# A fused attention and MoE kernel on one core: v on a second DMA queue, a token-major last chunk, and a new order

## The chip, the core and the metric

The kernel runs on one core of one Trainium2 chip. The core has five engines, each with its own in-order instruction stream: TensorE (PE; its weight loads are listed apart as PEld), VectorE (DVE), ScalarE (ACT), GpSimd (POOL) and SyncE (SP). SP does no arithmetic here; it issues DMA transfers, and ACT can issue them too. The metric is the device time of one execution in microseconds (us), and the number to compare is the median of several runs. A profile is one execution taken apart; its own span is a little shorter than its time, since the time holds what lies around the program.

## What is computed

Two layers follow each other. The first is a linear attention: q and k are each projected by two small matrices S1 and S2 (8 x 32), and the outer product of the two projections (64 numbers) takes the place of q or k. The second is a gated layer over 4352 tokens, with 2048 hidden units and one beta for each.

```python
def phi(x):
    a = np.einsum('rd,bhsd->bhsr', S1, x)
    b = np.einsum('rd,bhsd->bhsr', S2, x)
    return np.einsum('bhsi,bhsj->bhsij', a, b).reshape(*x.shape[:-1], r * r)
q_p, k_p = (phi(q), phi(k))                      # batch 4, heads 4, 1088 tokens, 32 wide
kv = np.einsum('bhsf,bhsd->bhfd', k_p, v)
z = np.sum(k_p, axis=2)
num = np.einsum('bhsf,bhfd->bhsd', q_p, kv)
den = np.einsum('bhsf,bhf->bhs', q_p, z)[..., None] + 1e-06
...
h = x @ w_in                                     # x: 4352 x 128, w_in: 128 x 2048
g = h * (1.0 / (1.0 + np.exp(-beta * h)))
return g @ w_out                                 # w_out: 2048 x 128
```

## The kernel before

The kernel scales w_in by beta and w_out by 1/beta once (`winp`, `woutp`, in 16 bits), so that the gated layer becomes a product, a silu and a product.

**The order.** The program is written out by hand as a list of short names, `SEQ` (line 842). Each name is a function that issues a few instructions; the list is walked once, at the end of the kernel. Every engine runs its own instructions in the order of the list, and semaphores keep the data dependences. So the list decides, for each engine, what stands behind what.

**Names.** The digit after the letters is the batch, a second digit a part of it. Small letters and capitals of the same name are the same work on different engines.

- Loads: `lk`, `lq`, `lv` bring k, q and v of a batch (`load_rows` line 143, `load_v` line 158), `lb` beta spread over all partitions, `li` w_in, `lo` w_out, `lp` beta for `woutp`, `l1` and `l2` S1 and S2. All go through SP's queue, except `l1`. v is loaded in four pieces of 32 partitions each.
- `h` is one idle matmul into a part of a PSUM tile that nobody reads (line 263); `ci`, `c0`, `c1` make constants.
- `sm` spreads S over the partitions (line 283), `sk` multiplies it with a 0/1 mask for pairs of heads (DVE, line 300), `sw` copies it, `s2` makes blocks of S2.
- k: `tk` transposes k of a batch on DVE (line 446), `kp` projects it on PE (line 465), `ka` transposes the result back (line 516), `o` (POOL) and `O` (DVE) make the outer products in five parts (line 488). `gr`, `gc`, `wp`, `wm`, `wc` make from k the weights of the denominator.
- q: `tq`, `qp`, `qa` in the same way, `DM`/`dm`, `DR`, `DI`, `DS`/`ds` multiply, sum, invert and scale for the denominator (capitals on DVE, small on POOL), `p` (POOL) and `P` (DVE) make the outer products, `t` transposes them on DVE (line 700).
- kv: `v` accumulates k's outer products with v on PE (line 774 for batch 0, line 745 for the others), `kt` and `kc` take it out of PSUM, `nd` deals it to other partitions by six transfers on SP's queue.
- The attention output: `n` (line 715; for batch 0, `f` turns the outer products with PE, `m`/`M` copy them, and `n0` is line 828), and `x` (ACT) or `X` (DVE) copies it into `xT`, the gated layer's input (lines 726 and 840).
- The gated layer: tokens are cut into ten chunks of 256 or 512. `W` is a wave (line 384): two or four units of 128 hidden channels into a PSUM tile of 1024 columns, of which there are two. `S` is its silu on ACT into a buffer `g` (line 401), `V` the second product (line 416), accumulated over all 16 units, with w_out stationary and g moving. `y` transposes a finished chunk on DVE (line 434), and `z` stores it in pieces of 32 partitions, 128 bytes for each token and piece (line 360). There are 68 W, 68 S and 68 V. `u`/`U` make `winp` (line 324), `g`, `e`, `a` make `woutp` on POOL, DVE and ACT.

The first wave needs `x00` and the first half of `winp`; the first V needs the first four blocks of `woutp`; a chunk of batch 1 needs `n1`.

Of the kernel before, what the change touches and what calls it, by code (L numbers as in the profile page):

```python
# [19 lines left out]
def kernel(  # L20
# [39 lines left out]

# [97 lines left out]
    def load_v(b):  # L158
# [3 lines left out]
        for g in range(4):  # L162
            nj = min(NJK, T - NJK * g) if b == B - 1 else NJK
            SP.dma_start(
# [134 lines left out]
    def pair_s():  # L299
        DVE.tensor_tensor(  # L300
            out=sk, in0=cut(sps["t"], [[R, 2], [0, 2], [1, R]]), in1=cut(hm, [[0, 2], [R, 2], [1, R]]), op=MUL
        )
# [50 lines left out]
    def store(o_sb, t0, nt, queues):  # L353
        c = t0
        while c < t0 + 32 * nt:
# [3 lines left out]
            for g4 in range(4):  # L359
                queues[g4 % len(queues)].dma_start(  # L360
# [37 lines left out]
    def silu():  # L398
        ci, j0, jn, per, tw, wv = moe["silu"].pop(0)
        g = sbG.tile([P, 2, TCH], F16, tag="g", name="g")  # L400
        ACT.activation(out=g, in_=wv, func=ACTF.Silu)  # L401
# [7 lines left out]
    def w2():  # L409
        ci, j0, jn, g = moe["todo"].pop(0)  # L410
        t0, tw = tok_chk[ci]
        if j0 == 0:
            moe["acc"] = one("moeout") if ci in ALT else acc("moeout")
        for jj in range(jn):
            j = j0 + jj
            PE.matmul(  # L416
                out=moe["acc"][:, :tw],
                lhsT=woutp[:, j, :],
                rhs=g[jj],
                start=(j == 0),  # L420
                stop=(j == NJ - 1),
            )
# [6 lines left out]
    def turn_out():  # L429
# [4 lines left out]
        DVE.transpose(out=o_sb[:, :nt, :].rearrange("p t d -> p (t d)"), in_=t[:, :tw])  # L434
# [455 lines left out]
```

## Time and profile before

| | us |
|---|---|
| median of 3 runs | 113.21 |
| the runs | 113.64, 110.37, 113.21 |
| the profiled execution's own time | 112.63 |
| its span | 110.8 |
| PE busy in the span | 100.0 |
| ACT busy | 73.5 |
| DVE busy | 63.4 |
| POOL busy | 33.1 |
| mean TensorE clock that was granted | 0.961 of full |

The page of the profile gives the busy time of each engine and, in 40 equal slices of the span, its tenths. Three other views are used: busy time in stretches that one chooses, instructions in order of time (start, duration, engine, line, operation, output and inputs, count; in brackets the idle time before it and what ended it), and the chain of waits, which follows the work that ended last back to the start. Groups of instructions give a count, the busy time, the mean of one in nanoseconds, and the idle time before them. Matmuls are pipelined: a row of a PE group can show more time for one than the distance between two.

### The profile page before, as it was taken

The page shows a single profiled execution, that of the slowest core. Times are in us where ns is not written, and L with a number is a line of the kernel's source. Part 1 is how long each engine was busy: PE and PEld are TensorE (multiplying, and loading weights), DVE is VectorE, ACT ScalarE, POOL GpSimd, SP SyncE. Part 2 cuts the span into 40 slices and gives each one's busy share as a digit, 9 for nine tenths or more (in the row PEclk, how much of TensorE's full clock was granted, in tenths as well). Part 3 has the DMA queues.
Part 4 walks back from the last instruction along what each step waited for, and adds up shares of the span by engine and source line. Part 5 has one row for each costly group of instructions (what it writes and reads, how often), then busy time and mean ns, then how long its engine had stood idle before and what let it go on. Part 6 is the DMA issues. An engine that isn't in the chain of part 4 may idle for free.

```text
span 110.8 us, 2848 instructions
## 1 busy us (share of the span) xinstructions
PE 100.0 (90%) x1183; PEld 55.1 (50%) x1183; DVE 63.4 (57%) x117; ACT 73.5 (66%) x89; POOL 33.1 (30%) x47
## 2 busy tenths in 40 slices
PE   6997779667999988999999999999999999999940
PEld 3453347154274564565755445565545555555730
DVE  3337899999779899909699878375220020020210
ACT  5000001337388993399979966999968999999920
POOL 5000940998009960540681018600000000000000
PEclk9999999975599999999999999999999999999996
DMA  3899999998920100599930015000143405014053
GB/s 84 252 286 214 229 411 321 223 228 254 380 105 6 25 16 6 76 300 213 167 54 10 18 18 87 8 0 11 22 72 61 69 6 94 0 25 70 0 92 50
DMA packets 24316, 12.64 MB, mean 114 GB/s; under 512 B 20464, under 2 KB 22512, under 8 KB 24304
## 3 DMA queue, kind: packets, MB, share of 16 engines
q1 hardware_dynamic: 23744, 12.40, 47.1%
q8 instruction: 9, 0.15, 0.6%
q10 hardware_dynamic: 560, 0.07, 0.4%
q14 instruction: 3, 0.02, 0.1%
HBM read 9.94 MB, written 2.23 MB: 110 GB/s over the span
## 4 chain that ended last, share of the span: by engine, by line
PE 58%; DMA 20%; DVE 15%; issue 1%; SPq 1%; DVEq 0%
PE moeout L416 24%; PE wave L384 23%; DMA beta_bc<-in_moe_beta_dram 11%; DMA v<-in_v_dram 9%; PE nps L715 5%; DVE woutp L338 3%; PE nps L828 2%; DVE qo L488 2%; DVE winp L324 2%; DVE kp L488 2%; PE kps L465 1%; DVE qt L700 1%; PE kvs L745 1%; DVE o_sb L434 1%; DVE qT L446 1%
## 5 line engine op out<-in xcount | busy, mean ns | idle before, releaser
L401 ACT ACTIVATE g<-wave 128x1024 f16<-128x1024 f32 x68 | 65.0, 1049 | 9.7 <-PE wave L384 9.1
L384 PE MATMUL wave<-xT,winp 128*128 128x512 f16 (+1 forms) x160 | 42.2, 362 | 0.7 <-DVE winp L324 0.7
L416 PE MATMUL moeout<-g,woutp 128*128 128x512 f16 (+1 forms) x160 | 38.2, 347 | 0.4 <-DVE woutp L338 0.2
L384 PEld LDWEIGHTS <-winp 128*128 128x128 f16 x160 | 21.3, 147 | 16.2 <-issue 4.3
L434 DVE STREAM_TRANSPOSE o_sb<-moeout 128x512 f32<-128x512 f32 (+1 forms) x10 | 6.3, 632 | 31.8 <-PE moeout L416 31.8
L416 PEld LDWEIGHTS <-woutp 128*128 128x128 f16 x160 | 15.2, 97 | 12.8 <-issue 1.4
L488 POOL TENSOR_TENSOR kp<-kab 128x512 f32<-128x512 f32 (+1 forms) x13 | 15.0, 1174 | 13.9 <-DVE kab L516 8.9
L263 PE MATMUL kvz<-idle 128*128 128x384 f16 x35 | 9.5, 428 | 1.1 <-DVE hm L234 1.1
L488 POOL TENSOR_TENSOR qo<-qab 128x512 f32<-128x512 f32 (+1 forms) x7 | 8.3, 1207 | 6.5 <-DVE qab L684 6.4
L488 DVE TENSOR_TENSOR qo<-qab 128x512 f32<-128x512 f32 (+2 forms) x10 | 10.0, 1003 | 0.1
L700 DVE STREAM_TRANSPOSE qt<-qo 128x512 f32<-128x512 f32 (+1 forms) x12 | 8.7, 742 | 0.0
L542 ACT COPY gt<-gram 128x32 f32<-128x32 f32 x3 | 0.6, 188 | 9.8 <-PE gram L531 9.8
L446 DVE STREAM_TRANSPOSE kT<-k 128x1088 f32<-128x1088 f32 x4 | 5.2, 1297 | 3.0 <-DMA k<-in_k_dram 3.0
L263 PEld LDWEIGHTS <-idle 128*128 128x128 f16 x35 | 4.0, 124 | 5.4 <-issue 3.7
L488 DVE TENSOR_TENSOR kp<-kab 128x512 f32<-128x512 f32 (+1 forms) x7 | 5.7, 807 | 0.0
L446 DVE STREAM_TRANSPOSE qT<-q 128x1088 f32<-128x1088 f32 x4 | 5.2, 1294 | 0.5 <-DMA q<-in_q_dram 0.5
L726 ACT CAST xT<-nps 128x576 f16<-128x576 f32 x6 | 3.8, 638 | 2.3 <-PE nps L715 2.2
L715 PE MATMUL nps<-qt,nd 32*32 32x288 f32 x192 | 5.3, 412 | 0.0
L666 POOL TENSOR_TENSOR qm<-qab 128x288 f32<-128x288 f32 x2 | 1.6, 803 | 12.2 <-DVE qab L660 12.2
L800 PE MATMUL qfps<-ident,qo 128*128 128x128 f32 x18 | 3.2, 314 | 1.8 <-DVE qab L660 1.8
L660 DVE STREAM_TRANSPOSE qab<-qps 128x576 f32<-128x576 f32 x6 | 4.4, 755 | 0.1
L745 PEld LDWEIGHTS kvs<-kp,v 128*32 128x32 f32 x216 | 3.2, 110 | 1.5 <-issue 1.5
(77 smaller groups left out, 67.6 us busy)
## 6 DMA issues: line engine op xcount, KB each, us to landing
k<-in_k_dram SPq DMA_DIRECT2D x4, 544.0 KB, 7.2
q<-in_q_dram SPq DMA_DIRECT2D x4, 544.0 KB, 9.4
v<-in_v_dram SPq DMA_DIRECT2D x15, 144.0 KB, 7.9
...
```

The source lines that it names most:

```text
L263: PE.matmul(out=kvz[:, P:], lhsT=idle, rhs=cut(idle, [[0, 3], [1, P]]), start=fresh, stop=True, skip_group_check=True,)
L384: PE.matmul(out=wv[:, jj // per, o : o + tw], lhsT=unit(j0 + jj), rhs=xT[:, t0 : t0 + tw], start=True, stop=True,)
L401: ACT.activation(out=g, in_=wv, func=ACTF.Silu)
L416: PE.matmul(out=moe["acc"][:, :tw], lhsT=woutp[:, j, :], rhs=g[jj], start=(j == 0), stop=(j == NJ - 1),)
L434: DVE.transpose(out=o_sb[:, :nt, :].rearrange("p t d -> p (t d)"), in_=t[:, :tw])
L446: DVE.transpose(out=dst[:, t0:t1].rearrange("p t s -> p (t s)"), in_=src[:, t0:t1].rearrange("p t d -> p (t d)"),)
L488: eng.tensor_tensor(out=cut(dst[b][:, j0:j1], [[F, n], [R, R], [1, R]]), in0=cut(t, [[step, n], [1, R], [0, R]], j0 * H * step), in1=cut(t ...
L660: DVE.transpose(out=cut(QAB[b], [[4 * R, 2], [4 * R * H, NJK], [1, 4 * R]], 2 * 4 * R * n), in_=PS["qps", b][n][:, :, :JW],)
L700: DVE.transpose(out=QT[b][:, j0:j1].rearrange("p j h c s -> p (j h c s)"), in_=QO[b][:, j0:j1].rearrange("p j h f -> p (j h f)"),)
L715: PE.matmul(out=tiles[g // 2][32 * h : 32 * h + 32, g % 2, : 32 * nj], lhsT=nd_of(b, h, fc, g), rhs=QT[b][rows, :nj, h, fc, :], start=(fc ...
L726: eng(out=cut(x0, [[32 * (QB[2 * i + 1] - QB[2 * i]), 2], [1, 32 * nj]]), in_=PS["num", b][i][:, :, : 32 * nj],)
L745: PE.matmul(out=KVZ[b][32 * h : 32 * h + 32, :F], lhsT=v_t[b][:, h, j, :], rhs=KP[b][:, j, h, :], start=(j == 0), stop=(j == NJK - 1), ski ...
```

## The change

The change has five parts.

1. **Loads.** v of batches 0 and 1 is issued by ACT (`lw0`, `lw1`) in place of SP; the pieces of 32 partitions of every batch come in the order 0, 2, 1, 3 in place of 0, 1, 2, 3. S2 is issued by ACT as S1 was.
2. **The mask of S.** `sk` is two ACT activations with the mask as scale, in place of one DVE product.
3. **The silu buffers.** 24 in place of 18.
4. **The last chunk.** Its silu writes tokens in another order, its second product has g stationary and w_out moving, 128 columns at a time into two PSUM tiles, so that a token lies on a partition; `y` is two DVE copies in place of a transpose, and `z` is two transfers on SP with 512 bytes for each token, in place of two on SP and two on ACT with 128 bytes.
5. **The order.** A new `SEQ`. Several pieces change their engine in it (`O01` to `o01`, `P00` to `p00`, `u0` to `U0` and so on).

```diff
-    sbG = ctx.enter_context(tc.tile_pool(name="sbG", bufs=18))
+    sbG = ctx.enter_context(tc.tile_pool(name="sbG", bufs=24))
...
-    def load_v(b):
+    def load_v(b, gs, eng):
...
-        for g in range(4):
+        for g in gs:
             nj = min(NJK, T - NJK * g) if b == B - 1 else NJK
-            SP.dma_start(
+            eng.dma_start(
...
-        DO[f"lv{b}"] = lambda b=b: load_v(b)
+        if b < 2:
+
+            DO[f"lw{b}"] = lambda b=b: load_v(b, (0, 2, 1, 3), ACT)
+        else:
+            DO[f"lv{b}"] = lambda b=b: load_v(b, (0, 2, 1, 3), SP)
...
     def load_s2():
-        SP.dma_start(out=sr[:, 1], in_=S2)
+        ACT.dma_start(out=sr[:, 1], in_=S2)
...
     def pair_s():
-        DVE.tensor_tensor(
-            out=sk, in0=cut(sps["t"], [[R, 2], [0, 2], [1, R]]), in1=cut(hm, [[0, 2], [R, 2], [1, R]]), op=MUL
-        )
+        for m in range(2):
+            ACT.activation(
+                out=sk[:, :, m, :],
+                in_=sps["t"][:, : 2 * R].rearrange("p (n r) -> p n r", n=2),
+                func=ACTF.Copy,
+                scale=hm[:, m, :1],
+            )
...
-    ALT = {len(tok_chk) - 3, len(tok_chk) - 1}
+    LAST = len(tok_chk) - 1
+    ALT = {LAST - 2}
...
-        ACT.activation(out=g, in_=wv, func=ACTF.Silu)
+        if ci == LAST:
+            ACT.activation(
+                out=cut(g, [[P, 2 * TCH // P], [1, 4], [4, 32]]),
+                in_=cut(wv, [[P, 2 * TCH // P], [32, 4], [1, 32]]),
+                func=ACTF.Silu,
+            )
+        else:
+            ACT.activation(out=g, in_=wv, func=ACTF.Silu)
...
+        if ci == LAST:
+
+            if j0 == 0:
+                moe["acc"] = (two("moeout")[:, 0], one("moeout"))
+            for n in range(tw // P):
+                for jj in range(jn):
+                    j = j0 + jj
+                    PE.matmul(
+                        out=moe["acc"][n][:, :P],
+                        lhsT=g[jj][:, n * P : n * P + P],
+                        rhs=woutp[:, j, :],
+                        start=(j == 0),
+                        stop=(j == NJ - 1),
+                    )
...
+        if ci == LAST:
+            for n in range(tw // P):
+                DVE.tensor_copy(out=o_sb[:, 4 * n : 4 * n + 4, :].rearrange("p t d -> p (t d)"), in_=t[n][:, :P])
+            outs.append((ci, o_sb, t0, nt))
+            return
...
-        store(o_sb, t0, nt, [SP, ACT] if ci == len(tok_chk) - 1 else [SP])
+        if ci < LAST:
+            store(o_sb, t0, nt)
+            return
+        b, r = divmod(t0, S)
+        for n in range(nt // 4):
+            SP.dma_start(
+                out=bass.AP(
+                    tensor=out.tensor,
+                    offset=out.offset + (b * S + r // 32 + 4 * n) * DM,
+                    ap=[[T * DM, 32], [DM, 4], [1, DM]],
+                ),
+                in_=o_sb[:, 4 * n : 4 * n + 4, :],
+            )
```

The order, old and new, up to the attention output of batch 1 (`n1`) and a little beyond:

```diff
-        l1 lk0 l2 ci h0 c0 tk0 h h h h h h h h h h h h h h h c1 h h h sm sw1 sw0 lk1 sk lq0 s2 tk1 h h h
-        h kp0 ka0 o00 tq0 h h h h h o03 h h h kp1 gr0 lv0 gc0 h h wp0 ka1 O01 wm0 qp0 lq1 qc0 lb0 v00
-        qa0 qd0 li0 DMa li1 o02 v01 v02 DRa DIa v03 DSa gr1 P00 tq1 gc1 o04 lb1 DMb h wp1 wc1 v04 DRb f0
-        qp1 DIb m0 DSb kc n00 P01 o10 qa10 P02 qa11 lv1 U2 lk2 U3 h DM1 P03 lp DR1 x00 f1 DI1 u1 u0 m1 W
-        f2 W S W m2 S n01 W o11 o13 S f3 S P04 vz f4 X01 o14 W M3 W v10 O12 v11 v12 S DS1 v13 S v14 p10
-        W p13 S tk2 M4 kt1 p11 lo0 W S kp2 t10 W n02 W rb ka2 X02 lo1 S g7 a0 e2 lq2 g1 S e3 g5 t11 g4 W
-        gr2 V W g6 g9 e8 GC2 lk3 g11 e15 S e12 nd1 a10 S e14 wp2 W WC2 V e13 tq2 V p12 V S t12 W qp2 y
-        t13 qa20 V S V qa21 V V dm2 o20 W n1 tk3 S x10 W V x11 V V W S V W S kp3 DR2 y z O21 ka3 W O23
...
+        l2 ci l1 h0 h h h h h lk0 h c0 c1 lq0 h sm h h h sk lk1 tk0 lw0 s2 h h h h sw1 h h h kp0 h h sw0
+        ka0 h h h tq0 h h gr0 h h o00 gc0 h O02 o01 h h h lq1 wp0 o04 wm0 h qp0 h qc0 tk1 qa0 lb0 h o03
+        qd0 DMa h DRa DIa DMb v00 dsa kp1 v01 h ka1 DRb h h h h gr1 DIb p00 dsb li0 gc1 f0 p03 p04 wp1
+        v02 wc1 lb1 v03 tq1 P01 m0 v04 P02 kc qp1 u1 li1 lp lw1 h qa10 O10 h U0 lk2 h n00 f1 f2 x00 qa11
+        lo0 U3 h lo1 o14 W h h m1 m2 W n01 U2 S W O11 S dm1 f3 lq2 X01 S W f4 rb o12 v10 DR1 S W v11 o13
+        S W v12 DI1 v13 v14 DS1 M3 S p10 lv2 W tk2 W g5 kt1 e0 g1 e7 g4 m4 kp2 n02 g2 S P12 W S W g3 h
+        x02 ka2 S gr2 tq2 S W g15 p13 GC2 S h wp2 t10 W g11 S WC2 e12 a9 V W e13 O20 g6 g14 S t13 V qp2
+        t12 v20 a10 o21 qa20 a8 v21 W p11 qa21 nd1 V t11 S V W O24 o22 n1 y S o23 v22 v23 v24 lk3 tk3 W
+        x10 z x11 V DM2 W S V S V W V DR2 W S V W S S kt2 DI2 V W DS2 V p20 S V t20 W y nd2 kp3 ka3 W
```

The rest of both orders goes on in the same manner and ends with the last S, the last V, `y` and `z`.

More of the change, by code (lines that the diff above doesn't have):

```diff
@@ L347, in invert_beta, with store @@
         DVE.reciprocal(out=rbeta, in_=beta_pu.rearrange("p i u -> p (i u)"))
-    ALT = {len(tok_chk) - 3, len(tok_chk) - 1}
+    LAST = len(tok_chk) - 1
+    ALT = {LAST - 2}
     moe = {"ci": 0, "w": 0, "acc": None, "silu": [], "todo": []}
-    def store(o_sb, t0, nt, queues):
+    def store(o_sb, t0, nt):
         c = t0
@@ L359, in store @@
             for g4 in range(4):
-                queues[g4 % len(queues)].dma_start(
+                SP.dma_start(
                     out=bass.AP(
@@ L411, in w2 @@
         t0, tw = tok_chk[ci]
[L412 to L422, printed above, removed]
+        if ci == LAST:
[11 more added lines that the diff above has]
+                    )
+        else:
+            if j0 == 0:
+                moe["acc"] = one("moeout") if ci in ALT else acc("moeout")
+            for jj in range(jn):
+                j = j0 + jj
+                PE.matmul(
+                    out=moe["acc"][:, :tw],
+                    lhsT=woutp[:, j, :],
+                    rhs=g[jj],
+                    start=(j == 0),
+                    stop=(j == NJ - 1),
+                )
         if j0 + jn == NJ:
@@ L439, in store_out @@
         ci, o_sb, t0, nt = outs.pop(0)
-        store(o_sb, t0, nt, [SP, ACT] if ci == len(tok_chk) - 1 else [SP])
+        if ci < LAST:
[3 more added lines that the diff above has]
+        for n in range(nt // 4):
+            SP.dma_start(
+                out=bass.AP(
[4 more added lines that the diff above has]
+                in_=o_sb[:, 4 * n : 4 * n + 4, :],
+            )
     PS, KP, QO, QT, ND, KAB, QAB, RC, GT, KVZ = ({} for _ in range(10))
@@ L848 @@
-        W p13 S tk2 M4 kt1 p11 lo0 W S kp2 t10 W n02 W rb ka2 X02 lo1 S g7 a0 e2 lq2 g1 S e3 g5 t11 g4 W
-        gr2 V W g6 g9 e8 GC2 lk3 g11 e15 S e12 nd1 a10 S e14 wp2 W WC2 V e13 tq2 V p12 V S t12 W qp2 y
-        t13 qa20 V S V qa21 V V dm2 o20 W n1 tk3 S x10 W V x11 V V W S V W S kp3 DR2 y z O21 ka3 W O23
-        DI2 S O24 o22 V S W V V lq3 S W lv2 V S W ds2 S v20 y v21 v22 v23 P20 v24 t20 P23 p22 W S V W
-        O30 V S kt2 V W V S W P21 gr3 W S V gc3 W t22 S lv3 wp3 S tq3 t23 V W V W t21 V WC3 z y S qp3 S
@@ L853 @@
-        W z o32 nd2 qa30 S V o31 qa31 V dm3 V W n2 V S V x20 x21 DR3 W V DI3 DS3 O34 S z P30 W S V W V W
-        v30 y v31 S W S t30 S o33 p32 P33 V W V W v32 v33 v34 S p31 W kt3 t33 nd3 S V W V z t32 S S W
-        t31 V W V S W S S V W V n3 y S x30 V x31 W V S z V W V S W V W V S W V S W V y S S W V S W S V W
-        V W V z S S W V W S S V W V S W S V W V S W V S W y V W V S S W V W V S W V S W S S V W V z S V
-        V V y z y z
+        l2 ci l1 h0 h h h h h lk0 h c0 c1 lq0 h sm h h h sk lk1 tk0 lw0 s2 h h h h sw1 h h h kp0 h h sw0
@@ new lines @@
+        x02 ka2 S gr2 tq2 S W g15 p13 GC2 S h wp2 t10 W g11 S WC2 e12 a9 V W e13 O20 g6 g14 S t13 V qp2
+        t12 v20 a10 o21 qa20 a8 v21 W p11 qa21 nd1 V t11 S V W O24 o22 n1 y S o23 v22 v23 v24 lk3 tk3 W
+        x10 z x11 V DM2 W S V S V W V DR2 W S V W S S kt2 DI2 V W DS2 V p20 S V t20 W y nd2 kp3 ka3 W
+        p22 V t22 S P21 p23 S t23 O30 W V S W gr3 S lq3 o33 W V S W gc3 V t21 vz tq3 n2 y S z x20 W V
+        lv3 x21 V V W V S W o34 S V W V S o31 wp3 S W O32 V W S WC3 V W v30 y v31 S qp3 qa30 V S W qa31
@@ L858 @@
+        V V W S W S V dm3 V S W v32 v33 DR3 DI3 v34 kt3 DS3 z S W S z V W V V y W S P30 P31 t30 W V S V
+        S W V V W V nd3 S S W p33 V W p32 V t31 S W S S V t33 t32 y n3 V x30 W V x31 S V W V S W V W S V
+        z W S V W V S W V S V S W V z S W V S W V W V S y z W V S W V S W S V y W V S S z W V W S V V S
+        W S V W V S W V W V S V V y S z V y z
     """
```

## The prediction

> **What bounds the kernel now.** I read the 40 slices first, then the engines' busy time in stretches, then the instructions in order of time.
>
> ```profile
> PE   6997779667999988999999999999999999999940
> DVE  3337899999779899909699878375220020020210
> ACT  5000001337388993399979966999968999999920
> POOL 5000940998009960540681018600000000000000
> PEclk9999999975599999999999999999999999999996
> DMA  3899999998920100599930015000143405014053
> ```
>
> Three stages show (slices of 2.77 us, counted from 0). Up to slice 10 the DMA engines are full and ScalarE (ACT) has little to do. From 8 to about 45 us VectorE (DVE) is at nine tenths. From 45 us TensorE (PE) is full, and at the very end ACT is too. The clock row has a dip in slices 8 to 10.
>
> ```profile
> 10.00:15.00 5.00, 2.95 (x67) 1.15 (x69) 4.54 (x9) 0.18 (x1) 3.97 (x4) 1.00 1.03 266
> 40.00:45.00 5.00, 4.33 (x56) 2.44 (x55) 5.00 (x9) 2.46 (x3) 0.72 (x1) 1.00 0.09 16
> 45.60:84.00 38.40, 38.28 (x548) 20.97 (x548) 24.11 (x37) 32.91 (x37) 11.80 (x11) 1.00 0.40 77
> ```
>
> The columns are PE, weight loads, DVE, ACT, POOL (GpSimd), clock, DMA share, GB/s. DVE is busy 4.54 and 5.00 of 5 us in the first two; PE 38.28 of 38.4 in the third. So the end is set twice: by when DVE has prepared batch 1, then by how much work PE has left.
>
> ```profile
> 1.06 6.02 PE L263 MATMUL kvz<-idle 128*128 128x384 f16 x19 [1.06 <-DVE hm L234]
> 4.66 1.31 DVE L446 STREAM_TRANSPOSE kT<-k 128x1088 f32<-128x1088 f32 x1 [2.46 <-DMA k<-in_k_dram]
> 8.34 0.71 PE L465 MATMUL kps<-kT,sk 64*32 64x288 f32 x16
> 10.14 0.81 DVE L516 STREAM_TRANSPOSE kab<-kps 128x288 f32<-128x288 f32 x2
> 15.48 2.06 PE L774 MATMUL kvz<-v,kp 128*64 128x32 f32 x64
> 23.57 0.87 PE L384 MATMUL wave<-xT,winp 128*128 128x256 f16 x4
> 24.80 2.17 DVE L324 TENSOR_TENSOR winp<-w_in_sb,beta_bc 128x512 f16<-128x512 f32 x2
> 45.59 1.60 PE L715 MATMUL nps<-qt,nd 32*32 32x288 f32 x64
> ```
>
> The milestones: the first wave at 23.57; the attention output of batch 1 (`n1`, line 715) at 45.59, just after DVE's last transpose for it. `n1` is my gate: at it the old order has issued 15 W and 8 V, the new one 15 W and 4 V (counted in the two orders).
>
> **The front: -2.6 us.** Start first. In the new order 18 idle matmuls stand ahead of `kp0`; at 6.02/19 = 0.317 us each from 1.06, plus some 0.6 for `sm`, `kp0` starts at 7.4 instead of 8.34 (S lands by then: its loads are first on ACT's queue). `tk1` (1.31) no longer stands ahead of `ka0`, which so ends near 8.9 instead of 10.95: 2.05 earlier, with 1.31 still owed, 0.7 net. Then DVE's load up to the gate:
>
> ```profile
> L488 DVE TENSOR_TENSOR qo<-qab 128x512 f32<-128x512 f32 x7 | 7.0, 1007 | 0.1
> L488 DVE TENSOR_TENSOR kp<-kab 128x512 f32<-128x512 f32 x5 | 4.9, 974 | 0.0
> L338 DVE TENSOR_TENSOR woutp<-w_out_sb,rbeta 128x128 f16<-128x128 f32 x7 | 3.3, 507 | 0.0
> L324 DVE TENSOR_TENSOR winp<-w_in_sb,beta_bc 128x512 f16<-128x512 f32 x2 | 2.2, 1126 | 0.1
> L666 DVE TENSOR_TENSOR qm<-qab 128x288 f32<-128x288 f32 x1 | 0.9, 912 | 0.0
> L840 DVE CAST xT<-nps 128x320 f16<-128x320 f32 x1 | 0.5, 492 | 0.4 <-PE nps L828 0.4
> L300 DVE TENSOR_TENSOR sk<-sps,hm 128x32 f32<-128x32 f32 x1 | 0.2, 192 | 1.8 <-ACT qw L309 1.8
> ```
>
> Off DVE go `DM1` (0.91), three woutp scalings (1.5), and six small ones between 0.19 and 0.49, some 2.1 together (`sk`, `DSa`, `DSb`, `M4`, `X02`, and the first `y`, now behind `n1`): 4.5. On it come `U0` (1.1) and four outer products (`O10 O11 P12 O20`, about 1.0 each) for four that leave (`P00 P03 P04 O12`), one of half size, others partly while POOL was idle; I put 1.1 on that swap. Net 4.5 - 2.2 = 2.3, with 0.7 a gate at 45.59 - 3.0 = 42.6. Against this stands that POOL, which takes what DVE gave, slows DVE's products (the 0.97 mean hides single ones of 0.7 and of 1.3): if each of the nine DVE products from `P01` to `O20` took 0.2 more, 44.4. I take 43.0, -2.6, nearer the first because slices 5, 6 and 10, 11 show POOL with room. Bounds: -4 (all room used) and 0 (POOL becomes what DVE was).
>
> W itself hardly starts earlier. I add up DVE's new order:
>
> ```profile
> 13.37 1.33 DVE L488 TENSOR_TENSOR kp<-kab 128x512 f32<-128x512 f32 x1
> 14.73 0.83 DVE L586 STREAM_TRANSPOSE qab<-qps 128x288 f32<-128x288 f32 x2
> L660 DVE STREAM_TRANSPOSE qab<-qps 128x576 f32<-128x576 f32 x6 | 4.4, 755 | 0.1
> ```
>
> From 8.9: `tq0` 1.3, `O02` 1.3, `wm0` 0.2, `tk1` 1.3, `qa0` 0.8, `qd0` and `DMa` to `DMb` some 1.7 make 15.5; `ka1` 0.8, `DRb` and `DIb` 0.7, `tq1` 1.3, `P01` and `P02` 1.3 each make 20.9; `qa10` 0.8, `O10` and `U0` 0.9 each make 23.5. So the first wave stays at 23.5 to 24. (The loads of win and beta are then long there: the old kernel had them for its use at 20 to 25.) On PE, `gr1`, `f0` and `wp1` follow `ka1`, then 40 of the kv instructions at 2.06/64 us, 1.3 together; `kc` comes near 19.2.
>
> ACT's new work: `sk` as two small activations near 4.4, before any other need for ACT: nothing on the path. Eight issues of v:
>
> ```profile
> 0.74 0.60 ACTq L212 DMA_DIRECT2D sr<-in_S_dram  x1
> 2.48 2.89 SPq L164 DMA_DIRECT2D v<-in_v_dram  x4
> ```
>
> At 0.60 each, `lw0` holds ACT 2.4 us behind `sk` (until 7.2; `gc0` needs `ka0` at 8.9), and `lw1` 2.4 us between `kc` (near 19.2) and `x00`, which so goes at 21.6 while W waits for `U0` at 23.5. Hidden, with 1.5 us of cover; at the old longest spacing SP paid, 2.89/4 = 0.72, still hidden. `m4`, `x02` and one woutp scaling come to ACT (1.1 together), which has room until 84 us. SP is freed of eight issues. The 24 silu buffers do nothing: in the orders silu never leads V by more than 11 before and 12 after, under 18.
>
> **From the gate to the last V: +0.8.** Before, this takes 106.65 - 45.59 = 61.06.
>
> ```profile
> 72.35 0.58 PE kvs L745 x32
> 76.96 0.43 PE wave L384 x2
> 77.39 0.43 PE moeout L416 x2
> 95.15 0.49 PE wave L384 x2
> 84.62 21.36 ACT L401 ACTIVATE g<-wave 128x1024 f16<-128x1024 f32 x23
> 104.64 2.00 PE L416 MATMUL moeout<-g,woutp 128*128 128x256 f16 x16
> 106.67 0.45 DVE L434 STREAM_TRANSPOSE o_sb<-moeout 128x256 f32<-128x256 f32 x1 [1.60 <-PE moeout L416]
> 107.16 0.89 ACTq L360 DMA_DIRECT2D out_dram<-o_sb  x2
> ```
>
> Four V more are owed: 4 x 0.43 = +1.7. The first two parts of batch 2's kv, 32 of its 72 instructions, are done ahead of `n1`: -0.6. The end of the old kernel is bound by ACT (23 silus in a row, 0.93 each), which stretches a wave's pair from 0.43 to 0.49: 23 x 0.05 = 1.2. In the new order ACT is 7 silus ahead of V at `n3`, not 4, with 21 W and 28 V left: PE 21.1 us, ACT 21 x 0.93 + 1.3 = 20.8. PE binds again: -1.2. The last chunk's 16 matmuls of 256 columns (2.00 us, 0.125 each) become 32 of 128, each with its own weight load: between 0 (half the columns, half the time) and +2.0 (no faster each). No row shows one; I take +0.9, the middle. Sum 1.7 - 0.6 - 1.2 + 0.9 = +0.8: last V at 43.0 + 61.06 + 0.8 = 104.9, -1.8.
>
> The Trainium skill ("TensorE: Matmul & The Clock Gate", Back-to-back issue gap) gives about 81 ns for a sustained matmul of 128 columns with its load; by it the 32 would take 2.6 us and the term be +0.6. No row here shows it.
>
> **The tail: -0.3.** The transpose of 0.45 becomes two copies of half the size, the first under PE's last matmuls: -0.2. Two issues on SP stand for two on each of two queues, and packets of 512 B for 128 B: between -0.4 and +0.5 (one issue, 0.45); I take -0.1. The permuted silu output of the last chunk is put at nothing, with a bound of +0.9 (the last silu twice as long).
>
> Sum: -1.8 - 0.3 = -2.1. The profiled execution took 112.63 (span 110.8, 1.83 around it); 112.63 - 2.1 = **110.5**. The median shown is 113.21, of runs from 110.37 to 113.64, so the forecast is 2.4% below the median and 1.9% below the profiled run. About 2% is what a measurement of this kernel can tell from no change.
>
> **Rivals.** *v comes late: slower.* In the new order PE meets `v00` ahead of `kp1`, so all of batch 1 waits for batch 0's v.
>
> ```profile
> 2.48 9.64 DMA v<-in_v_dram
> 9.00:10.00 1.00, 1.00 (x15) 0.61 (x8) 1.00 (x1) 0.00 (x0) 0.00 (x0) 1.00 1.11 207
> 15.00:16.00 1.00, 1.00 (x26) 0.54 (x21) 0.94 (x3) 0.00 (x0) 0.19 (x1) 1.00 1.11 442
> ```
>
> While v moved the engines gave 207 GB/s, after it 442, both with full engines. `ka1` has its turn on DVE at 15.5; `v00` (0.45) and `kp1` (0.72) must precede it, so v has until 14.4. v is issued at 4.8 to 7.2. If both queues got equal bytes, 0.59 MB of v and 0.59 of the others at 207 take 5.7: v is there near 12. If they alternate run by run (1152 B of v, 4352 of k or q, by the lines that load them), 32 pairs for each of 16 engines at 207/16 GB/s take 13.6: from 7.2, 20.8. The old kernel's first product with v stands at 15.48; I take 14. Later, each us costs one: the gain is lost from 16.5, and from 19.4 the median is passed by 2%; at 20.8 the time is 110.5 + 6.4 = 116.9. For it: the full DMA row. Against: the batch-1 loads behind k and q start later than before, and the pieces now alternate halves of the partitions.
>
> The Trainium skill ("DMA: Bandwidth & Descriptors", Issuing engines are not separate DMA queues) says that transfers from ACT and SP run on the same engines and interleave, and that only issue time is saved. That speaks for this rival; the trace, with one small load on ACT's queue, cannot show it.
>
> *The front gains nothing that PE keeps: within 2%.* Gate and V owed cancel: POOL's load eats 1.5 of the 2.3, and the end stays ACT-bound. -2.6 + 1.5 + 1.2 = +0.1 in place of -2.6 in these terms: 112.4 to 113.
>
> *All room is used: much faster.* Gate at -4 and the short matmuls free: 110.5 - 1.4 - 0.9 = 108.2; the clock dip, which more idle matmuls may fill, could give another half us.
>
> **How the numbers follow.** The forecast (109 to 112) 0.45; nothing kept 0.30; more gained 0.11; v late 0.14. The forecast lies on both sides of 110.95, the median less 2%: 0.31 of it faster. Faster 0.31 + 0.11 + 0.02 = 0.44; slower 0.13 of the last; the rest, 0.43, the same. The range leaves out the ends of the two outer cases: 107.5 to 114.8; the forecast's own is 109 to 112.
>
> **What would show it.** `n1` near 43 and the last V near 105; 32 matmuls of about 0.09 in the last chunk; v's first product before 15; waves after 95 us back at 0.43; DVE full to 43 and POOL fuller from 15 to 40. The prediction is wrong if PE idles ahead of line 774, if POOL's outer products are waited for by `t11`, or if ACT still runs without a gap at the end.

## The result and the profile after

The changed kernel takes 123.75 us (median of 4 runs, 122.45 to 124.73), the kernel before on the same chip 112.48 (4 runs, 110.37 to 113.64): a ratio of 1.105, 95% interval 1.074 to 1.136. It is slower by 11 us, where the prediction said 110.5. The profiled execution took 124.49 us, its span 122.7. Medians are of all runs, while ratios and intervals leave out the runs in which the chip was in a slower state (so 1.105 is not 123.75 / 112.48), and where no interval is given too few others were left.

The 40 slices of the changed kernel, of 3.07 us each:

```profile
PE   6894750999799995799996999999999999983630
DVE  3218190397999899972499203519620200102010
ACT  4100100021789994589895897799979999999940
POOL 4006704078578997019081000243000000000000
PEclk9999995589999999999999999999999999999975
DMA  4999999204920151031675200320504050130501
```

Two holes are new. In slice 6 (18.4 to 21.5 us) PE and DVE stand still and POOL is at 4, while the DMA row is full. In slices 36 and 37, PE falls to 3 and 6 while ACT stays at 9. Busy time in stretches (PE, weight loads, DVE, ACT, POOL, clock, DMA share, GB/s) puts numbers to them:

```profile
10.00:15.00 5.00, 2.37 (x37) 1.13 (x35) 2.15 (x5) 0.43 (x3) 4.22 (x4) 1.00 1.00 319
17.00:21.00 4.00, 0.06 (x1) 0.00 (x0) 1.31 (x6) 0.00 (x0) 1.40 (x2) 0.72 1.04 360
104.00:119.00 15.00, 10.04 (x73) 6.60 (x71) 1.73 (x3) 13.81 (x9) 0.00 (x0) 0.96 0.22 35
```

From 10 to 15 us DVE works 2.15 of 5 us, where it worked 4.54 before; from 17 to 21 PE works 0.06 of 4 us; from 104 to 119 PE works 10 of 15 and ACT 13.8. The instructions in order of time (as before) name both causes. First the front:

```profile
5.78 7.06 ACTq L163 DMA_DIRECT2D v<-in_v_dram  x3
8.60 0.72 PE L512 MATMUL kps<-kT,sk 64*32 64x288 f32 x16
13.19 0.38 PE L578 MATMUL gram<-kab 128*32 128x32 f32 x18 [2.63 <-ACT qw L316]
21.18 1.07 PE L821 MATMUL kvz<-v,kp 128*64 128x32 f32 x16 [4.12 <-DMA v<-in_v_dram]
23.50 0.85 DVE L563 STREAM_TRANSPOSE kab<-kps 128x288 f32<-128x288 f32 x2 [5.02 <-PE kps L512]
32.10 0.63 PE L392 MATMUL wave<-xT,winp 128*128 128x256 f16 x4 [0.77 <-DVE qab L707]
50.92 1.67 PE L762 MATMUL nps<-qt,nd 32*32 32x288 f32 x64
```

The issues of v hold ACT until 12.84, not 7.2. The first product with v (`v00`) comes at 21.18, after a wait of 4.12 us for v; before it stood at 15.48. The held ACT is in this too: `gram` waited 2.63 us for the copies behind v's issues, and without the wait for v PE would have come to `v00` at 17.06, 8.5 us after `kp0`. In the kernels below that load v on SP's queue it is 5.7 to 7.7. `kp1` stands behind it on PE, so DVE's `ka1` comes at 23.50 in place of 15.5 in my walk. The first wave is at 32.10 (before 23.57) and `n1` at 50.92 (before 45.59). The chain of waits, read back from the first waves, has two pieces of v in it:

```profile
5.40 7.11 DMA v<-in_v_dram
12.53 8.52 DMA v<-in_v_dram
```

The two pieces join at 12.5 because the kernel's transfers, on both queues together, use eight completion semaphores in turn, and a transfer is issued only when the one eight places before it has landed (read from the trace's semaphore events). v's third piece so waited for k of batch 1 (landed at 7.88) and its fourth for its own first piece (landed at 12.51). The fourth landed at 21.05. Now the end:

```profile
92.38 16.11 ACT L416 ACTIVATE g<-wave 128x1024 f16<-128x1024 f32 x17
108.64 9.31 ACT L410 ACTIVATE g<-wave 128x1024 f16<-128x1024 f32 x4
113.44 0.60 PE L392 MATMUL wave<-xT,winp 128*128 128x256 f16 x4 [1.26 <-ACT g L410]
118.01 1.03 PE L434 MATMUL moeout<-woutp,g 128*128 128x128 f16 x8 [1.65 <-ACT g L410]
```

Seventeen silus take 16.11 us (0.95 each), the last four, of the same 128 x 1024 elements with the permuted output, 9.31 us (2.33 each). Waves wait for them (1.26 us in the row above; a PSUM tile comes free only when its silu is done), and so do the last products.

So the loss has two places, and one measure keeps them apart. Up to `n1` the front counts; from `n1` to the end of the last V, the end. In the changed kernel the second stretch is 119.04 - 50.92 = 68.1 us, before it was 61.06.

### The profile page after: what moved, and what is told of

Same layout as the page of the kernel before. It is cut to its first block, busy times and chain, and to the rows that moved or that the text cites. A ratio compares the mean times of both kernels' runs of the same rounds, so it can differ in the third digit from the quotient of the medians.

```text
span 122.7 us, 2904 instructions
## 1 busy us (share of the span) xinstructions
PE 101.7 (83%) x1212; PEld 57.7 (47%) x1212; DVE 59.1 (48%) x108; ACT 80.3 (65%) x94; POOL 37.1 (30%) x53
## 4 chain that ended last, share of the span: by engine, by line
PE 55%; DMA 15%; DVE 12%; ACT 10%; ACTq 2%; issue 2%; DVEq 0%
PE wave L392 20%; PE moeout L446 19%; DMA v<-in_v_dram 13%; ACT g L410 6%; ACT g L416 4%; PE nps L762 4%; DVE kp L535 3%; DVE qt L747 3%; PE kvz L821 3%; DMA sr<-in_S_dram 2%; PE kvs L792 2%; ACTq L932 2%; DVE woutp L345 2%; DVE qab L707 2%; PE kps L512 2%
## 5 line engine op out<-in xcount | busy, mean ns | idle before, releaser
L416 ACT ACTIVATE g<-wave 128x1024 f16<-128x1024 f32 x64 | 61.2, 1034 | 6.8 <-PE wave L392 6.2
L392 PE MATMUL wave<-xT,winp 128*128 128x512 f16 (+1 forms) x160 | 40.5, 351 | 4.2 <-ACT g L410 2.5
L446 PE MATMUL moeout<-g,woutp 128*128 128x512 f16 (+1 forms) x144 | 36.0, 356 | 0.0
L446 PEld LDWEIGHTS <-woutp 128*128 128x128 f16 x144 | 13.9, 97 | 12.3 <-issue 1.1
L535 POOL TENSOR_TENSOR qo<-qab 128x512 f32<-128x512 f32 (+2 forms) x11 | 13.0, 1194 | 10.6 <-DVE qab L731 10.5
L266 PE MATMUL kvz<-idle 128*128 128x384 f16 x48 | 13.5, 419 | 1.1 <-DVE hm L237 1.1
L410 ACT ACTIVATE g<-wave 128x1024 f16<-128x1024 f32 x4 | 9.3, 2534 | 0.1
L563 DVE STREAM_TRANSPOSE kab<-kps 128x288 f32<-128x288 f32 x8 | 3.4, 462 | 8.2 <-PE kps L512 8.2
L821 PE MATMUL kvz<-v,kp 128*64 128x32 f32 x72 | 3.5, 256 | 4.1 <-DMA v<-in_v_dram 4.1
L535 DVE TENSOR_TENSOR qo<-qab 128x512 f32<-128x512 f32 x6 | 5.9, 1003 | 0.0
L821 PEld LDWEIGHTS kvz<-v,kp 128*64 128x64 f32 x72 | 3.1, 175 | 5.4 <-issue 5.4
```

The source lines that it names most:

```text
L266: PE.matmul(out=kvz[:, P:], lhsT=idle, rhs=cut(idle, [[0, 3], [1, P]]), start=fresh, stop=True, skip_group_check=True,)
L392: PE.matmul(out=wv[:, jj // per, o : o + tw], lhsT=unit(j0 + jj), rhs=xT[:, t0 : t0 + tw], start=True, stop=True,)
L410: ACT.activation(out=cut(g, [[P, 2 * TCH // P], [1, 4], [4, 32]]), in_=cut(wv, [[P, 2 * TCH // P], [32, 4], [1, 32]]), func=ACTF.Silu,)
L446: PE.matmul(out=moe["acc"][:, :tw], lhsT=woutp[:, j, :], rhs=g[jj], start=(j == 0), stop=(j == NJ - 1),)
L535: eng.tensor_tensor(out=cut(dst[b][:, j0:j1], [[F, n], [R, R], [1, R]]), in0=cut(t, [[step, n], [1, R], [0, R]], j0 * H * step), in1=cut(t ...
L821: PE.matmul(out=kvz[64 * c : 64 * c + 64, 32 * m : 32 * m + 32], lhsT=KP[0][:, j, h, :], rhs=v_t[0][:, h, j, :], start=(j == 0 and m == 0) ...
```

## The experiments

The two theories were tested by undoing each alone and both together, then by looking for the mechanism inside each. All times are us. "v00", "n1" and "last V" are starts of the first product with v and of batch 1's attention output, and the end of the last V, in the profiled run.

| run | kernel | median (runs) | before there | ratio, 95% interval | v00 | n1 | n1 to last V |
|---|---|---|---|---|---|---|---|
| before | | 112.48 (4) | | | 15.48 | 45.59 | 61.1 |
| after | | 123.75 (4) | 112.48 | 1.105, 1.074 to 1.136 | 21.18 | 50.92 | 68.1 |
| e1 | after, last chunk as before | 119.21 (4) | 111.67 | 1.068, 1.055 to 1.081 | 23.02 | 51.70 | 62.2 |
| e2 | after, v on SP's queue | 116.14 (4) | 111.67 | 1.041, 1.031 to 1.051 | 15.44 | 43.09 | 67.7 |
| e3 | after, both | 111.08 (10) | 111.67 | none | 13.31 | 40.96 | 62.2 |
| e4 | before, token-major last chunk alone | 116.75 (4) | 111.67 | 1.047, 1.036 to 1.058 | 15.50 | 44.52 | 66.7 |
| e5 | e1, v first on ACT's queue | 112.51 (4) | 111.36 | 1.011, 1.004 to 1.018 | 15.16 | 43.82 | 62.2 |
| e6 | e1, copies ahead of v's issue | 120.97 (4) | 111.36 | 1.087, 1.079 to 1.095 | 22.51 | 52.74 | 62.2 |
| e7 | e2, silu plain, store permuted | 111.23 (4) | 111.36 | none | 14.62 | 42.26 | 62.2 |
| e8 | e2, silu reads permuted | 110.27 (4) | 111.36 | 0.987, 0.977 to 0.997 | 14.16 | 41.81 | 62.2 |
| e9 | e8, 18 buffers | 110.94 (6) | 112.08 | 0.991, 0.980 to 1.001 | 15.04 | 42.69 | 62.2 |
| e10 | e8, pieces 0, 1, 2, 3 | 110.60 (6) | 112.08 | 0.987, 0.977 to 0.998 | 14.57 | 42.22 | 62.2 |
| e11 | before, e8's last chunk alone | 113.13 (6) | 112.08 | none | 15.77 | 45.52 | 61.5 |
| e12 | e8 again | 111.09 (6) | 112.08 | 0.999, 0.993 to 1.005 | 16.63 | 44.28 | 62.2 |
| e13 | e8, six idle matmuls fewer | 109.91 (12) | 111.43 | 0.992, 0.987 to 0.997 | 14.71 | 42.36 | 62.2 |
| e14 | e8 again | 110.46 (12) | 111.43 | 0.990, 0.979 to 1.001 | 14.02 | 41.67 | 62.2 |

### One part undone at a time (e1, e2, e3)

e1 takes part 4 back (plain silu, w_out stationary, transpose, stores of 128 bytes; the kernel before had the last of these on two queues, here all go through SP's). The condition is switched off in the silu, the product, the copies and the store; the first is shown:

```diff
-    ALT = {LAST - 2}
+    ALT = {LAST - 2, LAST}
...
-        if ci == LAST:
+        if False:
...
```

> The changed kernel with the last chunk computed and stored as before (silu without the permutation, w_out stationary, transpose, pieces of 128 bytes; all on SP). Theory A (two separate costs: v of batch 0 comes late, and the last chunk's four permuted silus take 2.3 us each instead of 0.93 while ACT bounds the end): the four silus go back to 0.93, 4 x 1.4 = 5.6 us come back, about 118 us; n1 stays near 50.9. Rival B (the long silus are covered by PE's work, and all of the loss is from the front): 122 or more.

e2 puts v back on SP's queue, at the same place in the order; e3 does both.

```diff
-            DO[f"lw{b}"] = lambda b=b: load_v(b, (0, 2, 1, 3), ACT)
+            DO[f"lw{b}"] = lambda b=b: load_v(b, (0, 2, 1, 3), SP)
```

> The changed kernel with v of batches 0 and 1 issued by SP at the same places of the order, pieces still 0, 2, 1, 3. Theory A: v of batch 0 then stands in SP's queue right behind the second k and lands near 12 to 14 us instead of 21; v00 starts by 15, ka1 by 17 instead of 23.5, n1 near 45 instead of 50.9; about 118 us. Rival C (the new order itself is slow, since POOL and DVE share work badly): v00 is early but n1 stays at 49 or later, 121.5 or more.

> The changed kernel with both: v on SP, and the last chunk as before. What is left of the change is the new order, the two mask activations, S2 on ACT and the 24 buffers. Theory A: the two costs add up, 123.75 - 5.6 - 6 = about 112, no difference from the kernel before within 2 %. Rival C (the order is slow by itself): 116 or more. The prediction's own view of the order, without the two costs: about 110.5.

The order of time of e1, then of e2, then of e3:

```profile
23.02 0.66 PE L821 MATMUL kvz<-v,kp 128*64 128x32 f32 x16 [0.88 <-DMA v<-in_v_dram]
93.17 20.03 ACT L416 ACTIVATE g<-wave 128x1024 f16<-128x1024 f32 x21
```

```profile
15.44 0.66 PE L821 MATMUL kvz<-v,kp 128*64 128x32 f32 x16
100.83 9.31 ACT L410 ACTIVATE g<-wave 128x1024 f16<-128x1024 f32 x4
```

```profile
40.96 1.67 PE L762 MATMUL nps<-qt,nd 32*32 32x288 f32 x64
101.12 2.00 PE L446 MATMUL moeout<-g,woutp 128*128 128x256 f16 x16
```

e1 keeps the late v and loses the slow silus (21 in 20.03 us, 0.95 each); e2 the reverse. From the medians, e1 gives back 123.75 - 119.21 = 4.5 us and e2 123.75 - 116.14 = 7.6; the sum is 12.1, and e3, with both, gives back 12.7. The kernel before read 112.48 beside the changed kernel and 111.67 beside these, so each difference holds to about 1 us. Within that the two costs are separate and add up, and nothing else in the change loses anything of their size: e3's median stands at the time of the kernel before. The forecasts of 118 for e1 and e2 were missed by 1.2 and 1.9 us in opposite directions.

### The late v: issue or rate (e5, e6)

ACT was held by its issues until 12.84, and `sw`, S's copies, stood behind them: `gram` waited 2.63 us for them. So two things could cost: what is queued behind v's issues on ACT, or v itself. e5 (made from e1) leaves v on ACT's queue but issues it right behind S's two loads; e6 (from e1) puts the copies `sw` ahead of v's issues. `gc0`, the copy of `gram`, stays behind them. The edits of e5 and then of e6:

```diff
-        l2 ci l1 h0 h h h h h lk0 h c0 c1 lq0 h sm h h h sk lk1 tk0 lw0 s2 h h h h sw1 h h h kp0 h h sw0
+        l2 ci l1 lw0 h0 h h h h h lk0 h c0 c1 lq0 h sm h h h sk lk1 tk0 s2 h h h h sw1 h h h kp0 h h sw0
```

```diff
-        l2 ci l1 h0 h h h h h lk0 h c0 c1 lq0 h sm h h h sk lk1 tk0 lw0 s2 h h h h sw1 h h h kp0 h h sw0
+        l2 ci l1 h0 h h h h h lk0 h c0 c1 lq0 h sm h h h sk lk1 tk0 sw1 sw0 lw0 s2 h h h h h h h kp0 h h
```

> As e1 (last chunk as before, v on ACT), but with v of batch 0 issued right behind S1, near 2 us, before SP's queue has filled. Compare with e1 (119.2). Theory A (v is late because it is issued behind 3 MB of SP's loads, and its later pieces because each waits for an earlier transfer to land): v lands by 12, v00 starts by 14, n1 near 42, about 112 us. Rival F (a load on ACT's queue gets too small a share beside SP's whatever the time of its issue): v lands after 15, n1 at 45 or later, 115 or more.

> As e1, but the two copies sw0 and sw1 stand ahead of the v issues on ACT, so that the gram of batch 0, which needs the PSUM tile that they free, is not held while ACT waits to issue v. Compare with e1 (119.2). Theory A: the gram runs near 10 instead of 15, but kp1 stands behind v00 and v is as late, so n1 and the time stay within 1 us. Rival G (what costs is ACT held by the issues): n1 2 us earlier or more, 117 or less.

In order of time, e5 and then e6:

```profile
1.67 3.62 ACTq L163 DMA_DIRECT2D v<-in_v_dram  x4
10.43 4.23 POOL L535 TENSOR_TENSOR kp<-kab 128x512 f32<-128x512 f32 x4 [8.29 <-DVE kab L563]
15.16 0.66 PE L821 MATMUL kvz<-v,kp 128*64 128x32 f32 x16 [0.72 <-POOL kp L535]
```

```profile
11.98 0.38 PE L578 MATMUL gram<-kab 128*32 128x32 f32 x18
14.55 0.18 ACT L589 COPY gt<-gram 128x32 f32<-128x32 f32 x1 [8.29 <-DMA v<-in_v_dram]
22.51 1.07 PE L821 MATMUL kvz<-v,kp 128*64 128x32 f32 x16 [5.23 <-DMA v<-in_v_dram]
```

In e6 `gram` came 3.9 us earlier than in e1 (15.83 there) and the time did not fall: it rose from 119.21 to 120.97. So the hold of the copies is covered by the late v. The whole hold is not priced by this, for ACT still came to `gc0` (`gt` above) at 14.55 only, and without the 5.23 us for v PE would have been at `v00` at 17.28, about as late as in the changed kernel. In e1's profile, the longest of its four executions, the hold nearly is the delay: `gram` waited 3.87 us for the copies, and of the time until `v00` at 23.02 only the last 0.88 us is a wait for v.

In e5 the four issues take 3.62 us without a wait, and the time is 6.7 us under e1's, though still above the kernel before (1.004 to 1.018). The pieces land at 8.6, 10.7, 13.2 and 15.1. `v00` starts 0.09 us after the last of them; the row names POOL, but POOL's outer products had ended at 14.66. So v still arrives last there (the rival had it landing after 15, the theory by 12), and yet the time is the theory's: landed at 15.1, it costs little. ACT's queue as such is slow, since the last piece took 10.1 us, and it landed 4.3 us later than the last in e2. What cost 7.6 us was the issue of v on it that late, beside a full queue on SP, with ACT held meanwhile. No run separates the late landing from the hold. The rate shows in the share of the packets. For the changed kernel from 7 to 12.5 us and then from 17 to 21 (q1 is SP's queue, q10 ACT's; packets, MB, share of 16 engines' time):

```profile
q1 hardware_dynamic: 424, 1.56, 82.9%
q10 hardware_dynamic: 200, 0.21, 13.8%
```

```profile
q1 hardware_dynamic: 371, 1.30, 90.2%
q10 hardware_dynamic: 126, 0.13, 11.8%
```

v moved one packet for two to three of SP's, and its packets are a third the size: 0.21 of 1.77 MB (12%) and 0.13 of 1.43 MB (9%). v's last piece of 144 KB took from 12.53 to 21.05, 8.5 us. In e2, with v in SP's queue, its pieces were issued by 4.8 and had landed by 10.8.

### The permuted silu: which side costs (e4, e7, e8)

e4 is the kernel before with part 4 of the change alone. e7 (from e2) has the plain silu and stores the tokens in the other order; e8 (from e2) keeps the permutation but moves the stride from the silu's output to its input.

```diff
-        if ci == LAST:
+        if False:
...
-                    ap=[[T * DM, 32], [DM, 4], [1, DM]],
+                    ap=[[DM, 4], [T * DM, 32], [1, DM]],
```

```diff
-                out=cut(g, [[P, 2 * TCH // P], [1, 4], [4, 32]]),
-                in_=cut(wv, [[P, 2 * TCH // P], [32, 4], [1, 32]]),
+                out=cut(g, [[P, 2 * TCH // P], [4, 32], [1, 4]]),
+                in_=cut(wv, [[P, 2 * TCH // P], [1, 32], [32, 4]]),
```

> The kernel before with part 4 alone: permuted silu, g stationary, two copies, two stores of 512 bytes a token. Theory A: the last four silus take about 2.3 each, ACT bounds the end there, so 112.5 + 5.6 = about 118. Rival B (covered by PE's work): within 1 us of the kernel before. Rival D (the silus are long in the changed kernel because of what PE does beside them there, not because of the permuted output): they stay near 1 us here.

> As e2 (v on SP, last chunk token-major), but the silu of the last chunk writes in order, and the two stores carry the permutation instead (dimensions of 4 and 32 swapped in the output's address). Compare with e2 (116.1) and e3 (111.1). Theory A: the silus go back to 0.93, 5 us come back: 110.5 to 111.5, and the token-major end is worth less than 1 us either way. Rival D (the long silus come from the stationary g and its two PSUM tiles): they stay at 2.3, 116.

> As e2, but the last chunk's silu reads PSUM in the permuted order (innermost 4 elements 32 apart) and writes g in order. Compare with e2 (116.1). If the scattered 16-bit write is what costs (theory A): silus near 1.0, about 111. Rival H (any innermost run of 4, on either side, costs): they stay above 1.8, 114 or more.

The last silus of e4, and then the last silus and products of e8:

```profile
101.15 9.37 ACT L403 ACTIVATE g<-wave 128x1024 f16<-128x1024 f32 x4
```

```profile
99.54 3.77 ACT L410 ACTIVATE g<-wave 128x1024 f16<-128x1024 f32 x4
101.96 2.02 PE L434 MATMUL moeout<-woutp,g 128*128 128x128 f16 x32
```

e4 shows the cost without any of the rest: 9.37 us for four, 5.1 us more than the kernel before. In e8 the same tokens in the same order come at 0.94 us for each silu: reading 32-bit PSUM with a stride of 32 elements costs nothing, writing 16-bit values with a stride of 4 elements costs 1.4 us for 1024 elements of each partition. The 9.31 - 3.77 = 5.5 us appear whole in the stretch from `n1` to the last V (67.7 in e2, 62.2 in e8). e7 has the plain silu too, and its median is the kernel before's; its two last stores took 2.5 us each from issue to landing, against 2.0 and 1.9 in e8.

### The small parts (e9, e10, e11, e12)

e9 and e10 change e8 in a number and a list; e11 is e4 with e8's silu; e12 is e8 again.

```diff
-    sbG = ctx.enter_context(tc.tile_pool(name="sbG", bufs=24))
+    sbG = ctx.enter_context(tc.tile_pool(name="sbG", bufs=18))
```

```diff
-            DO[f"lw{b}"] = lambda b=b: load_v(b, (0, 2, 1, 3), SP)
+            DO[f"lw{b}"] = lambda b=b: load_v(b, (0, 1, 2, 3), SP)
         else:
-            DO[f"lv{b}"] = lambda b=b: load_v(b, (0, 2, 1, 3), SP)
+            DO[f"lv{b}"] = lambda b=b: load_v(b, (0, 1, 2, 3), SP)
```

> The kernel of e8 (v on SP's queue, last chunk token-major with the silu reading permuted and writing in order) with 18 silu buffers in place of 24. The prediction's statement: silu never leads V by more than 12 in the new order, so buffers 19 to 24 are never needed: 110.3 us, the same as e8 within 1%. Rival, the buffers let ACT run ahead near the end: waves or silus wait for a free buffer, and the time is 111.5 or more.

> The kernel of e8 with v's four pieces of 32 partitions loaded in the order 0, 1, 2, 3 as before, in place of 0, 2, 1, 3. Theory that the order of the pieces does nothing: 110.3 us, v's last piece of batch 0 landed within 1 us of e8's, the same first product with v within 0.3 us. Rival, neighbouring pieces share DMA engines or memory ports and move more slowly (207 GB/s stood in the kernel before while v moved): v's last piece lands 2 us later or more, v00 moves to 17 or later, and the time to 112 or more.

> The kernel before (its loads, its order, 18 buffers) with the token-major last chunk alone, its silu reading PSUM permuted and writing in order: e4 with its slow write taken away. If the write's stride was all of e4's 5.1 us, its four last silus take 0.94 us each and the time is that of the kernel before, 111.4, or up to 1 less (the tail: 512-byte stores). Rival, the token-major chunk costs something else too (its stores land later, its 32 short matmuls): 112.5 or more. The difference to e12 on the same chip is what the new order with its mask on ACT and its piece order is worth: 2 us or more if the prediction's front term holds at the end, under 1 if the end eats it.

> The kernel of e8 once more, as it was, beside the three others. 110.3 us, 0.987 of the kernel before; if e8's gain was chance, 111.3 and a ratio of 1.0. n1 near 41.8, the last V near 104.

e9, e10 and e12 lie within 0.5 us of one another: the six buffers and the order of the pieces are worth nothing that these runs can tell (v's last piece landed at 11.6 in e10, at 11.5 in e12). e11, with the old loads and order, stands 2.0 us above e12 by the medians of six runs each, and 1.0 above the kernel before, where the theory had it equal. Its lowest run, 110.94, lies among e12's (110.75 to 112.47), and without an interval neither difference is shown. Its four silus take 0.96 us each, and its stretch from `n1` is 61.5, so the token-major chunk with a clean write costs or gains little.

e12's gain was smaller than e8's (0.999 against 0.987), in intervals that overlap. Its profile is of its longest execution, 112.47, and cannot explain the median, but it shows what moves one execution. In order of time, e12, and under it e3, which has the same front:

```profile
5.56 0.40 PE L286 MATMUL sps<-ident,sr 8*32 8x8 f32 x16 [1.76 <-DMA sr<-in_S_dram]
9.76 1.21 PE L512 MATMUL kps<-kT,sk 64*32 64x288 f32 x16
44.28 1.67 PE L762 MATMUL nps<-qt,nd 32*32 32x288 f32 x64
```

```profile
5.32 0.31 PE L286 MATMUL sps<-ident,sr 8*32 8x8 f32 x16 [1.51 <-DMA sr<-in_S_dram]
5.89 1.80 PE L266 MATMUL kvz<-idle 128*128 128x384 f16 x10
7.62 0.71 PE L512 MATMUL kps<-kT,sk 64*32 64x288 f32 x16
```

In e12 `sm` waited 1.76 us for S's second load (landed at 5.42; at 4.36 in e8), and the ten idle matmuls behind `sm`, 0.34 us each, carry this on to `kp0`, though k was transposed by 6.3. `n1` came at 44.28 against 41.81. But the late S is not enough: in e3 S was nearly as late, and `n1` came at 40.96, the earliest of all. There the ten idle matmuls took 0.18 us each and `kp0` 0.71 in place of 1.21, so PE ran faster from the start.

### An earlier start (e13, e14)

e13 takes six of these ten idle matmuls out; e14 is e8 once more on the same chip.

```diff
-        l2 ci l1 h0 h h h h h lk0 h c0 c1 lq0 h sm h h h sk lk1 tk0 lw0 s2 h h h h sw1 h h h kp0 h h sw0
+        l2 ci l1 h0 h h h h h lk0 h c0 c1 lq0 h sm h h h sk lk1 tk0 lw0 s2 h sw1 kp0 h h sw0
```

> The kernel of e8 with six of the ten idle matmuls that stand between S's spreading (sm) and the first projection (kp0) taken out. Theory that the front is delayed by these: S's second load lands at 4.3 to 5.4 us, sm waits for it, and the ten idle matmuls of 0.33 us stand behind it, so that kp0 comes at 8.5 to 9.8 where k's transpose is done by 6.6. With four left kp0 comes at 6.6 to 7.9, 1.9 earlier, v00 and n1 follow by as much, and the time is 1 to 2 us under that of e14. Rival, v or other loads bind next: v's first pieces land at 9 to 11, the attention output moves by less than 0.5 and the time is the same. Second rival, the idle matmuls hold the clock up: without them the granted clock dips as in the kernel before, and the time is that of e14 or more.

> The kernel of e8 and e12 as it is, to stand beside e13 on the same chip: 110.3 to 111.1 us, n1 between 41.8 and 44.3 by when S's second load lands.

In order of time, e13 and then e14:

```profile
7.00 1.21 PE L512 MATMUL kps<-kT,sk 64*32 64x288 f32 x16
8.15 2.42 PE L266 MATMUL kvz<-idle 128*128 128x384 f16 x7
42.36 1.67 PE L762 MATMUL nps<-qt,nd 32*32 32x288 f32 x64
```

```profile
8.33 0.72 PE L512 MATMUL kps<-kT,sk 64*32 64x288 f32 x16
8.98 1.31 PE L266 MATMUL kvz<-idle 128*128 128x384 f16 x7
41.67 1.67 PE L762 MATMUL nps<-qt,nd 32*32 32x288 f32 x64
```

`kp0` came 1.3 us earlier, less than the 1.9 expected, and `n1` did not. PE ran slowly for longer: `kp0` took 1.21 us in place of 0.72, and the seven idle matmuls behind it 0.35 each in place of 0.19. `gram` so started at 10.50 against 10.22, and DVE waited 1.67 us for what follows from it. The row of the granted clock says 1.00 in both kernels; only the durations of equal matmuls show it, and the trace's own record of the clock, which begins, at full speed, at 11.6 us in e13 and at 8.0 in e14 (ahead of its first record the row reads 1.00).

This has the look of the second rival, but it is not shown that the missing idle matmuls did it. e8, e12 and e14 are one kernel, and that record begins at 8.2, 12.4 and 8.0 us in them; e7 and e9, with all ten idle matmuls, have the slow `kp0` too (1.20 and 1.21). From `v00` to `n1` all nine profiles of this order with v on SP's queue take 27.64 or 27.65 us. What differs is when `v00` comes, and that goes with S and with the time at which PE reaches full speed: among the eight with ten idle matmuls the earliest, e3, has it from 3.9 us (`v00` at 13.31), the latest, e12, from 12.4 (16.63). e13 had it nearly as late as e12 and its `v00` 1.9 us earlier. Its profile is of the longest of its twelve executions (110.56 of 108.42 to 110.56), e14's of the second shortest (109.85 of 108.60 to 112.18), so the two rows of `n1` compare unlike executions. The Trainium skill ("TensorE: Matmul & The Clock Gate", Part 1: The HAM clock gate) has PE at half its clock until it has been busy for a window of some 3.4 us; these durations (0.35 against 0.19) agree with the half, while e13's PE worked without a gap from 4.72 to 10.5 us at the slow speed, longer than one such window.

By the medians e13 is 0.5 us under e14, with overlapping ranges, where 1 to 2 us were expected. e13 takes 0.992 of the kernel before (0.987 to 0.997), about 1% less; e8, e10 and e14 cannot be told from it. Against the changed kernel this is some 10% (0.992 / 1.105).

## Why the prediction was wrong

- **v's landing (taken at 14; the step that failed first).** The right rival was in the prediction, with 20.8 as its end; the last piece landed at 21.05. I chose 14 from the old kernel's first product with v, a row of another queue and another time of issue. The reason given against the rival, that the loads behind would start later, was wrong: with v out of SP's queue they went earlier, q of batch 1 at 2.16 (before: 5.41), beta at 3.00 (6.01) and w_in at 3.64 (8.90), and stood ahead of v. The other, the order of the pieces, moved nothing in e10. That 20.8 and 21.05 agree so well is luck: the rival let all four pieces be issued by 7.2 and alternate one to one at 207 GB/s, whereas the fourth could go only at 12.53, behind the landing of the first, and v moved one packet for two to three of SP's at 320 to 360 GB/s. The Trainium skill ("DMA: Bandwidth & Descriptors", Issuing engines are not separate DMA queues) says that ACT's and SP's transfers interleave on the same engines; the trace agrees (both queues in one stretch, 12% and 9% of the bytes for v), and that rule deserved more than the chance of 0.14.
- **What a late v costs (one us for each).** A little more: the profiled executions of e1 and e3 have `v00` 9.7 us apart and their times 10.7 (120.21 and 109.47), those of the changed kernel and e2 5.7 and 8.0. While PE waits its granted clock falls too: from 20 to 24 us of the changed kernel it is 0.50, and `v00` and `kp1` take 1.07 and 1.21 us there against 0.66 and 0.71 in e2.
- **`lw0` on ACT, 2.4 us, "nothing on the path".** The issues held ACT for 7.4 us, from 5.40 to 12.84, since two of them waited for semaphores. The size was wrong, and so were the words: `sw` and `gc0` stood behind the issues, and by the wait at `v00` they alone would have brought PE there at 17.06, in place of some 14.3 (`kp0` and e8's 5.69). This was hidden only because v came later still.
- **The permuted silu ("put at nothing, with a bound of +0.9").** The second failed step. It cost 1.4 us on each of four silus, in a stretch that ACT bounds: 5.5 us in the profile, 4.5 to 5.1 by the medians of e1 and e4. The bound counted the last silu only, at double length; all four grew to 2.5 times, and each delays the one behind it.
- **The gate (-2.6).** The sum came out for the rest of the change, once v is early, but not by its terms. Over the eight profiles with v on SP's queue and the ten idle matmuls (e2, e3, e7 to e10, e12, e14) `n1` stands at 42.4 in the mean (40.96 to 44.28), in the three with the old order and loads (before, e4, e11) at 45.2: -2.8. The first sub-step was wrong: `kp0` came at 8.60 and not at 7.4. Half of this is that `sm`, ahead of ten of the idle matmuls, waited 0.60 us for S, which I took as landed; the rest is `sm` itself and idle matmuls a little longer than counted. So the other terms must have given more than I took, and that the sum agrees is in part luck. One candidate is a dip of the granted clock to a half, which the three old profiles have somewhere between 16 and 31 us (slices 8 to 10 of the kernel before) and these eight have not; no run separates it.
- **From the gate to the last V (+0.8).** It is 62.2 in every kernel with the new order and fast silus, against 61.06: +1.1, but by other terms. The short matmuls (+0.9) cost 2.02 us for 32 (e8) against 2.00 for 16 twice as wide: nothing. The Trainium skill's figure for them ("TensorE: Matmul & The Clock Gate", Back-to-back issue gap) is 81 ns; here it was 63. The end free of ACT (-1.2) came about half: in the chain of waits the old kernel has some 18 waves stretched to 0.48 or 0.49, e8 eight. And PE, before busy without a gap, has holes in the new order, in these rows from 46 to 80 us of the kernel before and of e12:

```profile
46.00:80.00 34.00, 33.88 (x475) 18.83 (x443) 23.00 (x36) 29.86 (x34) 11.40 (x11) 1.00 0.39 76
```

```profile
46.00:80.00 34.00, 33.03 (x383) 18.46 (x381) 18.03 (x32) 29.33 (x33) 9.94 (x10) 1.00 0.29 63
```

- **The tail (-0.3).** Nothing seen: from the last V to the span's end it is 4.2 us in e8 as in the kernel before.
- **24 buffers, the mask on ACT, S2 on ACT (nothing).** e9 bears out the first, as far as its runs can tell. The other two were not run alone.
- **The sum.** With the two failed steps repaired a gain is left, but only about half of the forecast one or less: 2.4% below the median shown was forecast, and e8 and its repeats stand at 0.987, 0.999 and 0.990, e13 at 0.992. Of the 2.8 us at the gate, 1.1 are given back before the last V. Of the 13.3 us between 110.5 and 123.75, v is 7.6 and the silu 4.5 to 5.1; the rest is of the size of the gain that did not come.
